# Loading r and k of a chunk by heads (48 rows of 4 KB twice) instead of by columns (112 rows of 2 KB twice)

## The chip, the cores and the metric

The kernel runs on one core of a Trainium2 chip. The metric is the time of one execution on the device in microseconds (us). A row of the traces is one instruction or a group of them on an engine: PE is TensorE (PEld its weight loads), DVE is VectorE, ACT is ScalarE, POOL is GpSimd and SP is SyncE. SP, ACT and POOL also issue DMAs; a name with a small q (SPq, ACTq) is the queue of instructions in front of the engine.

## The reference

A linear attention with decay (batch 4, 8 heads, 768 steps, 48 channels per head) feeds a mixture of 8 experts, of which each token takes one. In short:

```python
for t in range(S):                                   # S = 768
    kt, vt, rt = (k[:, :, t], v[:, :, t], r[:, :, t])
    cur = np.einsum('bhd,bhe->bhde', u[None] * kt, vt)
    y[:, :, t] = np.einsum('bhd,bhde->bhe', rt, state + cur)
    state = w[None, :, :, None] * state + np.einsum('bhd,bhe->bhde', kt, vt)
...
e_idx = np.argmax(x @ w_gate, axis=1)                # x: y as 3072 tokens x 384
for e in range(E):                                   # E = 8
    h = np.maximum(x[mask] @ w1[e], 0.0)
    out[mask] = gate_w[mask, None] * eom[mask, e, None] * (h @ w2[e])
```

## The kernel before

The attention goes through 24 chunks (NT) of 128 steps of one batch entry, six chunks of time (NCH) for each of the four batch entries, the entries in turn. Within a chunk the steps are two halves of 64 (c = 0, 1), and the 8 heads are 4 pairs (q) of two heads (j = 0, 1).

A chunk's input is one block of the array `rkv`: 128 rows of 1792 floats. The first 512 columns are r transposed, the next 512 are k transposed, and then follow k and v by tokens, 384 each. In the transposed part a row is a channel: rows 0 to 47 are the channels of the even heads (j = 0), rows 64 to 111 those of the odd heads (j = 1), and rows 48 to 63 and 112 to 127 are zeros. Along a row the order is half, pair, step.

The tiles called `rk` (128 x 1024 floats, 4 KB per row) hold r and k transposed of a chunk; there are five (`RINGS`), so chunk i uses tile i % 5. The tiles `k` (four) and `v` (five) hold the rest. Chunks 0 to 4 are loaded into `rk` in one DMA each of all 128 rows ahead of the loop. Each later chunk is loaded in two DMAs of `load`, which is told a part n: n = 0 is r and n = 1 is k, in both cases rows 0 to 111 (48 + 64). The second stays clear of the last 16 zero rows, which nobody overwrites with anything but zeros.

The order of the instructions on every engine is written out by hand, and each engine takes them in that order. In iteration i of the loop (from L1479):

- POOL multiplies r and k of chunk i + 2 (`product`), and DVE scales r and k of chunk i + 3 by a table in place (`scale`, L297).
- PE does `strips` of chunk i + 1; then ACT issues the load of part 0 of chunk i + 5 (L1488) and the load of `k` of chunk i + 5 (L1493), and later the store of a finished chunk.
- PE does `intra` of chunk i (L399), after which SP issues the load of `v` of chunk i + 5 (L1513).
- PE does `state` of chunk i + 2 (L353), `scores` of chunk i + 1 for three pairs (L327, called at L1517), `inter` of chunk i + 1 (L389, L1520) and `scores` for the fourth pair (L1521). `scores` reads r and k, `inter` reads r.
- SP issues the load of part 1 of chunk i + 6 (L1528).

So both parts of a chunk are issued one after the other, part 1 at the end of one iteration and part 0 early in the next. Ahead of the loop SP issues part 1 of chunk 5 (L1459), behind `scores(0)`, `product(0)` and `inter(0)`. The routing of finished chunks (small steps on DVE and PE) is woven into the same iterations. Behind the attention the experts run one after the other, with PE as the busy engine; they use other tiles and other loads.

Of the kernel before, what the change touches and what calls it, by code (L numbers as in the profile page):

```python
# [20 lines left out]
B, H, S, D = 4, 8, 768, 48  # L21
C = 128
# [25 lines left out]
HB = 64  # L48
# [10 lines left out]
RINGS = {"rk": 5, "k": 4, "v": 5}  # L59
# [1219 lines left out]
def rwkv_top1_moe(ctx, tc, rkv, wu, wg, w1, w2, r, kk, v, w, u, out):  # L1279
# [11 lines left out]
    with ExitStack() as actx:  # L1291
# [6 lines left out]
        rings = {nm: [pin.tile([C, RKW if nm == "rk" else NAT], F32, name=f"{nm}_{n}") for n in range(RINGS[nm])] for nm, (a, z) in PARTS.items()}  # L1298

        def load(nm, i, n=None, eng=nc.sync):  # L1300
            if i < NT:
                a, z = PARTS[nm]
                rows, at = slice(0, C), 0
                if n is not None:
                    rows, at, a, z = slice(0, HB + D), 512 * n, a + 512 * n, a + 512 * (n + 1)
                eng.dma_start(rings[nm][i % RINGS[nm]][rows, at : at + z - a], rkv[i, rows, a:z])

        for nm, i in (("rk", 0), ("k", 0), ("rk", 1), ("v", 0), ("k", 1), ("rk", 2), ("v", 1), ("k", 2)):
            load(nm, i)
# [14 lines left out]
        for nm, i in (("v", 2), ("rk", 3), ("k", 3), ("v", 3), ("rk", 4), ("v", 4)):  # L1324
            load(nm, i)
# [126 lines left out]
        make_fold(tc, rw, k)  # L1452
        att.state(0)
        load("k", RINGS["k"])
        att.causal(0)
        att.carry(0, 0)
# [195 lines left out]
```

## Time and profile before

| | us |
|---|---|
| median of three runs | 376.56 |
| lowest and highest of them | 375.86, 376.89 |
| the profiled execution | 372.32 |
| its span, first to last instruction | 370.5 |
| granted clock of TensorE, mean over the span | 0.98 of full |

The page lists the busy time of each engine and then cuts the span into 40 slices of 9.3 us. Each digit is the busy share of a slice in tenths. A wait is put down to what ended it; "issue" means that the engine waited for nothing that the profile shows. DMA shares are shares of 16 DMA engines' time. Times in timelines and windows are us from the start of the span.

### The profile page before, as it was taken

To read this page: it belongs to the slowest core of one execution; us is meant where nothing else is said; L and a number is where in the kernel's file an instruction comes from. 1 tells how busy PE (TensorE), PEld (TensorE's weight loads), DVE (VectorE), ACT (ScalarE), POOL (GpSimd) and SP (SyncE) were. 2 spreads that over 40 slices of the span, in tenths; PEclk is the share of its full clock that TensorE was granted. 3 is DMA by queue.
4 is the path that set the end of the run, shared out by engine and by line. 5 is a ranking of instruction groups with operands and counts; after the bars stand their busy time and mean duration, and the time that the engine had idled before them with its cause. 6 is when DMAs were issued, how large, how long until landed. Compare 5 with 4: busy or idle time off the path is not lost. (4 is left out here: it accounts for less than half of the span.)

```text
span 370.5 us, 12089 instructions
## 1 busy us (share of the span) xinstructions
PE 339.0 (92%) x4821; PEld 313.7 (85%) x4821; DVE 208.3 (56%) x481; ACT 179.0 (48%) x542; POOL 156.6 (42%) x229
## 2 busy tenths in 40 slices
PE   6699888889889889899999999999999999999990
PEld 2587776778777779889999999999999999999990
DVE  6566666857858428666446616624834835736500
ACT  3476654645646754265346434615535545535400
POOL 4968766746657575426005215223122132411021
PEclk9999999989989999999999999999999999999997
DMA  7968767767784351637526435633633734835010
GB/s 268 322 188 259 217 188 211 237 175 222 222 248 152 103 168 40 233 93 229 185 84 197 138 103 160 203 103 100 218 128 113 231 127 128 294 108 153 15 48 21
DMA packets 28850, 61.40 MB, mean 166 GB/s; under 512 B 4157, under 2 KB 13395, under 8 KB 28784
## 3 DMA queue, kind: packets, MB, share of 16 engines
q1 hardware_dynamic: 17120, 38.29, 33.2%
q10 hardware_dynamic: 8336, 12.60, 10.8%
q0 software_dynamic: 3328, 9.64, 8.2%
q8 instruction: 40, 0.66, 0.7%
q14 instruction: 26, 0.21, 0.2%
HBM read 51.04 MB, written 9.70 MB: 164 GB/s over the span
## 5 line engine op out<-in xcount | busy, mean ns | idle before, releaser
L896 POOL DMA_INDIRECT out_dram<-yo,gi x28 | 29.8, 1063 | 107.4 <-ACT yo L893 41.6
L858 PE MATMUL ps_h<-xh,w1h 128*128 128x416 f32 (+6 forms) x192 | 65.5, 341 | 0.0
L859 PE MATMUL ps_h<-xl,w1h 128*128 128x416 f32 (+6 forms) x192 | 63.7, 332 | 0.0
L860 PE MATMUL ps_h<-xh,w1l 128*128 128x416 f32 (+6 forms) x192 | 63.6, 331 | 0.0
L772 DVE TENSOR_TENSOR w1l<-raw,w1h 128x768 fp32r<-128x768 f32 x28 | 26.2, 957 | 62.1 <-ACT w1h L771 62.1
L807 POOL DMA_INDIRECT xg<-x_d,gi x28 | 30.8, 1099 | 55.7 <-PE ps_z L881 40.1
L867 ACT ACTIVATE hh<-ps_h 128x416 fp32r<-128x416 f32 (+6 forms) x64 | 30.8, 484 | 33.9 <-PE ps_h L860 33.7
L414 ACT ACTIVATE vc<-v,cs 128x48 f32<-128x48 f32 x192 | 45.9, 322 | 0.1
L868 DVE SCALAR_TENSOR_TENSOR hl<-ps_h,hh 128x416 fp32r<-128x416 f32 (+6 forms) x64 | 34.3, 540 | 15.7 <-ACT hh L867 15.6
L858 PEld LDWEIGHTS ps_h<-xh,w1h 128*128 128x128 f32 x192 | 36.1, 188 | 0.3
L859 PEld LDWEIGHTS ps_h<-xl,w1h 128*128 128x128 f32 x192 | 36.2, 188 | 0.0
L860 PEld LDWEIGHTS ps_h<-xh,w1l 128*128 128x128 f32 x192 | 36.1, 188 | 0.0
L373 POOL TENSOR_TENSOR T<-Ts,sq 128x192 f32<-128x192 f32 x40 | 20.3, 508 | 35.4 <-DVE Ts L372 20.5
L879 PE MATMUL ps_z<-hh,w2h 128*128 128x416 f32 (+2 forms) x96 | 33.7, 351 | 0.0
L399 PE MATMUL ps_y<-v,A 64*64 64x64 f32 x768 | 30.0, 227 | 4.0 <-issue 2.6
L881 PE MATMUL ps_z<-hh,w2l 128*128 128x416 f32 (+2 forms) x96 | 33.3, 347 | 0.0
L880 PE MATMUL ps_z<-hl,w2h 128*128 128x416 f32 (+2 forms) x96 | 33.3, 347 | 0.0
L921 PE MATMUL ps_o<-w2h,hh 128*128 128x384 f32 (+2 forms) x96 | 32.9, 343 | 0.0
L923 PE MATMUL ps_o<-w2h,hl 128*128 128x384 f32 (+2 forms) x96 | 32.2, 336 | 0.0
L922 PE MATMUL ps_o<-w2l,hh 128*128 128x384 f32 (+2 forms) x96 | 32.2, 336 | 0.0
L399 PEld LDWEIGHTS ps_y<-v,A 64*64 64x64 f32 x768 | 26.0, 139 | 5.9 <-issue 3.8
L310 POOL TENSOR_TENSOR rk<-rk 128x512 f32<-128x512 f32 x24 | 30.5, 1273 | 0.0
(214 smaller groups left out, 693.1 us busy)
## 6 DMA issues: line engine op xcount, KB each, us to landing
raw<-in_w_dram SPq DMA_DIRECT2D x64, 384.0 KB, 3.3
v<-in_rkv_dram SPq DMA_DIRECT2D x24, 192.0 KB, 4.2
x_d<-x ACTq DMA_DIRECT2D x22, 200.0 KB, 3.4
rk<-in_rkv_dram SPq DMA_DIRECT2D x19, 224.0 KB, 3.4
rk<-in_rkv_dram ACTq DMA_DIRECT2D x19, 224.0 KB, 3.5
k<-in_rkv_dram ACTq DMA_DIRECT2D x19, 192.0 KB, 3.7
rk<-in_rkv_dram SPq DMA_DIRECT2D x5, 512.0 KB, 5.3
k<-in_rkv_dram SPq DMA_DIRECT2D x5, 192.0 KB, 5.2
```

Source lines behind the costliest of these rows:

```text
L399: nc.tensor.matmul(o, A[rows, j, q, :], self.values(i, rows, 2 * q + j), start=(i < B and c == 0 and q == 0), stop=(q == NP - 1), skip_gro ...
L414: nc.scalar.activation(vc[:, h, :], vt[:, h, :], AF.Copy, scale=cs[:, h : h + 1])
L858: nc.tensor.matmul(o, wh[:, j, fs], xh, start=(j == 0), stop=False)
L859: nc.tensor.matmul(o, wh[:, j, fs], xl, start=False, stop=False)
L860: nc.tensor.matmul(o, wl[:, j, fs], xh, start=False, stop=(j == KC - 1))
L868: nc.vector.scalar_tensor_tensor(hl, o, 0.0, hh, op0=ALU.max, op1=ALU.subtract)
L879: nc.tensor.matmul(o, wh, hh, start=(f == 0), stop=False)
L880: nc.tensor.matmul(o, wh, hl, start=False, stop=False)
L881: nc.tensor.matmul(o, wl, hh, start=False, stop=(f == FC - 1))
L921: nc.tensor.matmul(o, hh, wh, start=(f == 0), stop=False)
L922: nc.tensor.matmul(o, hh, wl, start=False, stop=False)
L923: nc.tensor.matmul(o, hl, wh, start=False, stop=(f == FC - 1))
```

## The change

Part n of `load` becomes a block of rows in place of a block of columns: n = 0 is rows 0 to 47 (the even heads) with both r and k, 4 KB per row, and n = 1 is rows 64 to 111 (the odd heads). The zero rows 48 to 63 are no longer written behind the first load of a tile; they keep their zeros. The number of DMAs, the engines that issue them and their places in the order stay.

```diff
         def load(nm, i, n=None, eng=nc.sync):
             if i < NT:
                 a, z = PARTS[nm]
-                rows, at = slice(0, C), 0
+                rows = slice(0, C)
                 if n is not None:
-                    rows, at, a, z = slice(0, HB + D), 512 * n, a + 512 * n, a + 512 * (n + 1)
-                eng.dma_start(rings[nm][i % RINGS[nm]][rows, at : at + z - a], rkv[i, rows, a:z])
+                    rows = slice(HB * n, HB * n + D)
+                eng.dma_start(rings[nm][i % RINGS[nm]][rows, : z - a], rkv[i, rows, a:z])
```

Here C is 128, HB is 64 and D is 48.

## Rows read from the trace of the kernel before

**Rows 1.** The page: busy time, and slices of PE and DMA.
```profile
PE 339.0 (92%) x4821; PEld 313.7 (85%) x4821; DVE 208.3 (56%) x481; ACT 179.0 (48%) x542; POOL 156.6 (42%) x229
...
PE   6699888889889889899999999999999999999990
...
DMA  7968767767784351637526435633633734835010
```

**Rows 2.** Windows: stretch, its length, busy per engine, clock, DMA share, GB/s.
```profile
20.00:33.00 13.00, 12.94 (x417) 10.98 (x413) 9.64 (x17) 9.17 (x41) 10.34 (x33) 1.00 0.77 234
33.00:107.00 74.00, 64.35 (x2123) 55.20 (x2123) 50.21 (x113) 41.60 (x191) 49.64 (x71) 0.97 0.72 217
107.00:127.00 20.00, 18.31 (x563) 15.78 (x558) 14.21 (x37) 12.90 (x58) 11.69 (x13) 0.95 0.46 146
```

**Rows 3.** PE's waits, 33 to 107 us (us, times, longest): first and last.
```profile
PE ps_cf L405 <- issue: 2.8, 2, 1.7
...
PE ps_y L389 <- issue: 0.4, 1, 0.4
```

**Rows 4.** PE's waits, 107 to 130 us: the longest.
```profile
PE ps_y L399 <- DVE A L333: 1.2, 2, 0.8
```

**Rows 5.** PE's timeline: start, duration, instruction, [idle before, ended by].
```profile
42.53 0.33 PE L399 MATMUL ps_y<-v,A 64*64 64x64 f32 x3
43.82 0.97 PE L399 MATMUL ps_y<-v,A 64*64 64x64 f32 x26 [0.96 <-issue]
...
78.36 0.65 PE L405 MATMUL ps_cf<-rk,uw 128*32 128x128 f32 x8 [1.69 <-issue]
...
104.67 0.55 PE L486 MATMUL ps_x<-ident,x 128*128 128x128 f32 x3 [1.21 <-issue]
```

**Rows 6.** DMA queues, 20 to 103 us: packets, MB, share of 16 engines.
```profile
q10 hardware_dynamic: 6928, 10.52, 40.5%
q1 hardware_dynamic: 4582, 7.20, 30.2%
q8 instruction: 19, 0.31, 1.6%
```

**Rows 7.** Windows around two drops of the granted clock.
```profile
78.30:81.70 3.40, 3.34 (x43) 2.86 (x45) 1.06 (x2) 1.64 (x9) 2.34 (x3) 0.50 0.39 121
...
104.50:109.00 4.50, 4.33 (x108) 4.30 (x109) 1.35 (x4) 2.96 (x13) 2.01 (x2) 0.62 0.94 270
```

**Rows 8.** SP's timeline, 10 to 20 us.
```profile
11.31 0.37 SPq L1306 DMA_DIRECT2D rk<-in_rkv_dram  x1
16.18 0.34 SPq L1306 DMA_DIRECT2D v<-in_rkv_dram  x1
19.77 0.33 SPq L1306 DMA_DIRECT2D rk<-in_rkv_dram  x1
```

**Rows 9.** Line 1306 on ACT: duration in ns, minimum, median, maximum.
```profile
L1306 ACTq EVENT_SEMAPHORE  x36: 17/17/38, 14.8 to 105.3; - x36
L1306 ACTq DMA_DIRECT2D rk<-in_rkv_dram x19: 334/334/390, 14.9 to 103.6; - x19
```

**Rows 10.** SP's waits, 10 to 108 us (us, times, longest).
```profile
SPq L1306 <- PE ps_a L327: 26.4, 17, 3.1
```

**Rows 11.** PE's timeline at inter(0).
```profile
12.02 0.68 PE L389 MATMUL ps_y<-T,rk 48*64 48x64 f32 x16 [1.24 <-DVE T L368]
```

**Rows 12.** ACT's timeline, second half of chunk 6.
```profile
20.17 0.33 ACTq L1306 DMA_DIRECT2D rk<-in_rkv_dram  x1
```

**Rows 13.** DVE's timeline, scale of chunk 6.
```profile
28.63 1.22 DVE L297 TENSOR_TENSOR rk<-rk,ps_tb 128x1024 f32<-128x1024 f32 x1
```

**Rows 14.** Tile rk, 13 to 107 us: time from issue to landing.
```profile
DMA to landing us min/median/max: 2.5/3.5/4.6
```

**Rows 15.** Line 297 (scale): idle before it (us, times) until this.
```profile
  DMA rk<-in_rkv_dram: 0.2, 1
```

**Rows 16.** DMA queues, 3 to 8 us: packets, MB, share of 16 engines.
```profile
q1 hardware_dynamic: 788, 1.92, 99.0%
```

## The prediction

> **What bounds the kernel now.** The page comes first [rows 1]. TensorE (PE) is busy 92% of the 370.5 us, but the slices differ: the first 18 hold 6 to 9 tenths, the others are full but for the last. All r and k loads are issued before 104 us, in the first twelve slices, so only idle time of PE in that stretch can change. The DMA slices are highest in the same stretch.
>
> Next come the windows [rows 2]. From 20 to 33 us PE is busy 12.94 of 13.00 us; from 33 to 107 us 64.35 of 74.00; from 107 to 127 us 18.31 of 20.00. The DMA shares are 0.77, 0.72 and 0.46. In the middle stretch every wait of PE is "issue", an engine that waits for nothing that the profile shows: 12 waits in six rows, 9.5 us [rows 3]. Behind 107 us none of PE's waits is of that kind; the longest is for DVE [rows 4]. The last reloads are issued at 103 us and land a few us later, so these waits end with the loads. One of them looks like this: PE stands idle 0.96 us in the middle of L399's matmuls, whose inputs were there for the three before [rows 5].
>
> The DMA view gives a candidate for what PE waits for. In 83 us queue q8, of kind "instruction", moved 19 packets of 0.31 MB in all, 16 kB each [rows 6]. PE's two rows in the middle stretch are 2123 instructions each, 4246 in 74 us [rows 2], and 19 packets in 83 us make 17 in 74 us: about 250 instructions to a packet. I read the 12 waits as instruction packets that come late because they share the 16 DMA engines with the loads. That is an inference from coincidence: from 20 to 33 us the DMA share was as high and PE waited for nothing.
>
> The Trainium skill, page "Runtime: NRT & Kernel Launch", section "Instruction fetch mechanics", says that instructions are refilled in 16 KiB blocks of 256 and that crossing a block is mostly hidden. The packet size agrees with the 16 kB of [rows 6]; "mostly hidden" does not agree with the 9.5 us of [rows 3], if my reading of them is right. By that rule the change would be worth nothing at all, 376.6 us; by the rows it is worth what the sum below says.
>
> PE's clock is part of it. From 78.3 to 81.7 us the granted clock was 0.50, the lower level of 1.2 GHz, and from 104.5 to 109 us it was 0.62 on average [rows 7]. Each drop follows an "issue" wait, of 1.69 us until 78.36 and of 1.21 us until 104.67 [rows 5], and costs 3.4 x 0.50 = 1.7 us and 4.5 x 0.38 = 1.7 us.
>
> **The change part by part.** *Issue.* 38 transfers before, 38 after, on the same queues at the same places: on SP the issues took 0.37 and 0.33 us for the 112 rows of rk and 0.34 us for the 128 of v [rows 8], on ACT a median of 334 ns for rk [rows 9], so no price by rows is visible. Nothing.
>
> *Waits of the transfers.* SP's reload at L1528 now overwrites r and k of one head of each pair instead of k of both. The last reader of either is the same: scores' last matmuls (L1521), behind inter (L1520). SP waits for that matmul already, 17 times, 26.4 us in all [rows 10]. ACT's reload finds its slot free: its semaphore instructions take 38 ns at most [rows 9]. Only the first SP reload (L1459) gains a wait: it was issued at 11.31 us, and inter(0), which reads r, starts at 12.02 and takes 0.68 us [rows 8, 11]. It moves by about 1.4 us; behind it on SP stands the v load, which waits for its own release until 16.18 us, so nobody is held up. Nothing.
>
> *Landing.* The shortest way from the second half's issue to its first reader is chunk 6: ACT issues at 20.17 us, scale reads at 28.63 us [rows 12, 13], 8.5 us, against 3.5 us median and 4.6 us at most to land [rows 14]. Scale waited for an rk transfer once in the whole execution, 0.2 us [rows 15]. So 3.9 us cover the slowest one; gone, each us would cost up to a us per chunk.
>
> *DMA work.* Per chunk 2 x 112 rows x 2048 B = 458.8 kB become 2 x 48 x 4096 = 393.2 kB, and 224 packets become 96. Over 20 to 103 us ACT's queue q10 took 40.5% of 16 engines for 10.52 MB, SP's q1 30.2% for 7.20 MB [rows 6]: 51.1 and 55.7 ns of one engine per kB. The reload costs 229.4 x (51.1 + 55.7) = 24.5 engine-us per chunk; at the same price per kB it will cost 21.0. All queues together spend about 960 engine-us on 17 chunks, 56.5 each, so the change takes 3.5, or 6%. No row shows a transfer into 48 partitions, so the price per kB has bounds. Low: the opening burst, where 4 KB rows are mixed with others, 99% of 16 engines x 5 us for 1.92 MB [rows 16], 41.3 ns per kB: 16.2 engine-us, -8.3 per chunk. High: each transfer now lands on one half of the partitions; if each half has ways of its own, and half the engines' rate goes through them, the price doubles: 42.0, +17.5. I take the middle value, the same queues' own price: both halves are issued 0.4 us apart (19.77 and 20.17 us [rows 8, 12]) and run side by side, so together they fill the partitions as before.
>
> *What PE gets of it.* 9.5 us of waiting at a DMA share of 0.72 and none at 0.46 make 36.5 us per unit of share [rows 2, 3]. A cut of 6% of 0.72 is 0.045: -1.6 us. From below it is 0, since 0.77 went without a wait for 13 us. I take the middle, -0.8 us.
>
> **The sum.** The profiled execution took 372.32 us, 1.8 us more than its span; less 0.8 it is 371.5. The three timed runs have a median of 376.56, 4.2 us above that execution, so executions of this kernel differ by more than the term; for the median the sum gives 375.8. A measurement of this kernel tells about 0.3% (1.1 us) from no change, so this is no measurable change.
>
> **The rivals.**
> *Faster: the waits shrink with the work.* For it: the waits end where the loads end [rows 3, 4]. Against: no wait at 0.77 [rows 2]. At the full slope -1.6 us; at the low price 15% of 0.72, -3.9 us; a clock drop that no longer comes gives 1.7 us more. 371 to 375 us. Chance 0.33.
>
> *Slower: half the partitions, dearer packets.* Its place is each reload between 20 and 107 us. From 62.3 ns per kB on (24.5 / 393.2), 17% above the loop's 53.4, the reload costs more engine time than before, and instruction packets come later. At half as much again: 31.5 engine-us, +12%, +3.3 us, and one more clock drop, 1.7 us: 381.6. Doubled: +31%, +8.1 us, 384.7. For it: nothing in the trace lands on so few partitions. Against: the halves overlap. Chance 0.23.
> Here the Trainium skill speaks against the change: "SBUF — State Buffer", section "Door 1: The DMA port swizzle", says that DMA bandwidth goes by how many of 16 ports the partitions reach, and that partitions 0 to 63 reach 8, 64 to 127 the other 8. No transfer here shows it. By it alone each half would take the doubled price, 384.7 us.
>
> *Slower: other drops.* Shifted packets make another long wait, and the clock falls once or twice more with no more DMA work: +1.7 to +3.4 us. Chance 0.05.
>
> *Slower: scale waits for a late half.* The landing would have to go from 3.5 to over 8.5 us; then up to a us per chunk for each us. Chance 0.02.
>
> **How the numbers follow.** No measurable change 0.37 (the likeliest; own range 375.4 to 377.7), faster 0.33, slower 0.23 + 0.05 + 0.02 = 0.30. The range goes from 372.8, a low price without a clock gain, to 380.5, most of the way to half as much again: it leaves out about one in ten on each side.
>
> **What would show it.** q1 and q10 lose 19 x 64 packets each, and 1.2 MB together. Scale still waits for no reload. The DMA share from 33 to 107 us is about 0.68; over 0.75 speaks for dearer packets, and the time to landing with it. PE's "issue" waits in that stretch stay within 8 to 10 us, with two clock drops. The prediction is wrong if these waits move by 2 us or more, if a drop goes or comes, or if waits appear on rk's landing.

## The result and the profile after

The changed kernel takes 376.75 us (median of 22 executions, 373.05 to 379.94) against 375.86 (369.56 to 380.73), a ratio of 1.0068 with a 95% interval of 1.0041 to 1.0094. The comparison leaves out every execution more than 1.5% above the fastest of its own kernel, which takes more from the kernel before because one of its executions took 369.56; over all 22 of each the medians differ by 0.24%. A second comparison on another chip gave 1.0030, 0.9990 to 1.0071. The change makes the kernel slower by something between nothing and 0.9%; a gain of more than 0.1% is excluded.

The forecast of 375.8 us started from three runs of the kernel before with a median of 376.56; over 22 executions that median is 375.86. So the forecast stood for 0.8 us less, and the kernel came out 0.9 us slower by the medians of all executions, some 2.6 us by the ratio.

The profiled execution of the changed kernel took 373.06 us, with a span of 371.1. PE and DVE execute as many instructions as before; only the two rk transfers have another shape. Its windows over the same stretches as [rows 2], with the same columns:

```profile
20.00:33.00 13.00, 12.71 (x410) 10.79 (x410) 9.21 (x16) 8.94 (x41) 10.53 (x34) 1.00 0.83 222
33.00:107.00 74.00, 64.82 (x2159) 55.27 (x2162) 50.33 (x113) 41.78 (x192) 49.52 (x71) 0.98 0.74 203
107.00:127.00 20.00, 17.28 (x528) 14.51 (x532) 13.96 (x36) 13.87 (x61) 12.54 (x14) 1.00 0.47 152
```

In the middle stretch fewer bytes move (203 GB/s for 217) and yet the DMA engines are busier, 0.74 for 0.72, where the prediction said about 0.68; from 20 to 33 us 0.83 for 0.77. The DMA queues from 20 to 103 us, beside [rows 6], say which:

```profile
q10 hardware_dynamic: 5833, 9.96, 44.4%
q1 hardware_dynamic: 3526, 6.67, 28.6%
```

The share times 16 engines times 83 us, divided by the bytes, is 59.2 ns of one engine per kB on ACT's queue, where it was 51.1, and 56.9 on SP's, where it was 55.7; for both queues together 58.3 for 53.0. A second execution of the changed kernel (after_again, below) gives 59.4 for both. Over the whole execution the page counts 64 packets fewer for each of 19 transfers on either queue (before: 17120 on q1 and 8336 on q10):

```profile
q1 hardware_dynamic: 15904, 37.67, 33.2%
q10 hardware_dynamic: 7120, 11.98, 11.7%
```

PE's waits from 33 to 107 us (us in all, times, longest), beside [rows 3]. All that are "issue":

```profile
PE ps_cf L405 <- issue: 3.4, 2, 2.0
PE ps_y L399 <- issue: 2.7, 5, 0.9
PE ps_a L353 <- issue: 1.4, 4, 0.8
PE ps_x L486 <- issue: 1.0, 1, 1.0
PE ps_y L389 <- issue: 0.7, 1, 0.7
```

That is 9.2 us in 13 waits, where the kernel before had 9.5 in 12. But the same view from 107 to 130 us now holds two rows of this kind, where the kernel before had none [rows 4]:

```profile
PE ps_y L389 <- issue: 1.5, 2, 1.2
PE ps_cf L500 <- issue: 0.9, 1, 0.9
```

With 0.2 us from 20 to 33 us this makes 11.8 us instead of 9.5. Summed from 8 to 140 us it is 12.1 for 10.3, and 11.1 in after_again. PE's clock still falls twice to its lower level of 1.2 GHz, the first time at the same place as in [rows 7], the second time later (the middle window shows the place where it fell before):

```profile
78.30:81.70 3.40, 3.22 (x39) 2.74 (x40) 0.64 (x2) 1.01 (x6) 1.90 (x2) 0.51 0.24 63
104.50:109.00 4.50, 3.86 (x127) 3.42 (x127) 2.59 (x8) 3.08 (x13) 3.16 (x4) 1.00 0.99 266
129.60:133.00 3.40, 3.40 (x40) 2.83 (x39) 1.63 (x8) 2.40 (x8) 0.76 (x2) 0.51 0.85 273
```

SP's timeline, beside [rows 8], has the first reload 1.3 us later and the v load behind it where it was:

```profile
12.61 0.34 SPq L1306 DMA_DIRECT2D rk<-in_rkv_dram  x1
16.03 0.34 SPq L1306 DMA_DIRECT2D v<-in_rkv_dram  x1
19.07 0.33 SPq L1306 DMA_DIRECT2D rk<-in_rkv_dram  x1
```

### The profile page after: what moved, and what is told of

The parts are those of the page before. It is cut to its first block, busy times and chain, and to the rows that moved or that the text cites. A ratio compares the mean times of both kernels' runs of the same rounds, so it can differ in the third digit from the quotient of the medians.

```text
span 371.1 us, 12073 instructions
## 1 busy us (share of the span) xinstructions
PE 340.3 (92%) x4821; PEld 314.1 (85%) x4821; DVE 208.6 (56%) x481; ACT 179.5 (48%) x542; POOL 158.0 (43%) x229
## 5 line engine op out<-in xcount | busy, mean ns | idle before, releaser
L807 POOL DMA_INDIRECT xg<-x_d,gi x28 | 31.6, 1127 | 54.9 <-PE ps_z L881 39.1
L310 POOL TENSOR_TENSOR rk<-rk 128x512 f32<-128x512 f32 x24 | 30.5, 1273 | 0.0
```

## The experiments

Theory 1 is the prediction's "half the partitions, dearer packets": a transfer into neighbouring rows of one half of the partitions costs more DMA time per byte, and instruction packets then reach PE later. Against it stand theory 2 (long packets: the size or number of the transfers costs), theory 3 (packets cost by their bytes and the difference is scatter), and the place of issue. Ratios are to the kernel before on the same chip, with 95% intervals; where the medians of all executions tell something else, they stand beside. In the edits HB is 64 and D is 48, and of long edits only the lines that matter are shown.

**micro: the transfers by themselves.** Nothing of the kernel is computed: only transfers run, eight of each shape from SP, then eight pairs of each from SP and ACT. All of a shape go into one place of one tile, so that on each queue one waits for the one before it. Rows and columns of part n:

```
cols:   slice(0, HB + D), slice(512 * n, 512 * (n + 1))     # 112 rows x 2 KB
heads:  slice(HB * n, HB * n + D), slice(0, RKW)            # 48 x 4 KB
rows:   slice(HB * n, HB * (n + 1)), slice(0, RKW)          # 64 neighbouring x 4 KB
step:   slice(n, C, 2), slice(0, RKW)                       # every second x 4 KB
all:    slice(0, C), slice(512 * n, 512 * (n + 1))          # 128 x 2 KB
```

> Transfers alone, nothing of the kernel's computation: for each of five shapes (112 rows x 2 KB, 48 rows x 4 KB, 128 rows x 2 KB, 64 rows x 4 KB taking every second row, 64 neighbouring rows x 4 KB), eight transfers one after the other from SP, then eight pairs of halves from SP and ACT at once. Theory 1 (half the partitions make packets dearer): 48 neighbouring rows alone take about twice the engine time per byte of 112 rows or of every second row, and 64 neighbouring rows likewise; in pairs the gap shrinks but stays. Theory 2 (long packets): 4 KB packets cost as much per byte as 2 KB packets in every shape. Theory 3 (scatter): as theory 2.

Some of the DMA issues of this program (tile, engine, count, KB each, median us from issue to landing):

```profile
all<-in_rkv_dram SPq DMA_DIRECT2D x8, 256.0 KB, 2.6
step<-in_rkv_dram SPq DMA_DIRECT2D x8, 256.0 KB, 2.9
rows<-in_rkv_dram SPq DMA_DIRECT2D x8, 256.0 KB, 3.4
...
cols<-in_rkv_dram SPq DMA_DIRECT2D x8, 224.0 KB, 2.6
...
heads<-in_rkv_dram SPq DMA_DIRECT2D x8, 192.0 KB, 2.8
```

These are the transfers one by one. For the same 256 KB, 64 spread rows take 0.3 us longer than 128 rows, and 64 neighbouring rows another 0.5. The 192 KB of 48 neighbouring rows land later than the 224 KB of 112. The DMA queues while the pairs run, first the two columns parts (124.81 to 148.05 us), then the two halves of heads (149.50 to 174.34 us):

```profile
q1 hardware_dynamic: 1024, 1.84, 26.9%
q10 hardware_dynamic: 1024, 1.84, 24.4%
...
q1 hardware_dynamic: 512, 1.57, 23.9%
q10 hardware_dynamic: 512, 1.57, 23.0%
```

Both queues' share times 16 engines times the stretch, over both queues' bytes, is 51.8 ns per kB for the columns and 59.4 for the heads: 15% more. Of 256 KB each, 64 neighbouring rows side by side cost 60.0 and 64 spread rows 51.5. Alone, from SP only, the columns cost 54.9, the heads 55.8, 64 neighbouring rows 56.1 and 64 spread rows 57.1 ns per kB, so theory 1's expectation of twice the price alone was missed. The higher price is one of two concentrated transfers side by side, which is how the loop runs them.

The rule of the Trainium skill that spoke against the change ("SBUF — State Buffer", section "Door 1: The DMA port swizzle": fewer ports reached, less bandwidth) agrees in the order of the landings, 3.4 us for 64 neighbouring rows against 2.6 for 128. Of the prediction's doubled price per kB nothing is seen in the engines' time: 60.0 ns against 51.5 is the widest gap in micro. The landing itself can't rule a doubling out, because most of it does not go with the bytes, as one transfer of the kernel before shows:

```profile
wu<-in_wu_dram SPq DMA_DIRECT2D x1, 4.0 KB, 1.9
```

Less these 1.9 us, 1.5 us stand against 0.7 (an estimate, from one transfer of 4 KB).

**cols128, heads64, step2: 128 rows' bytes in three shapes.** All three load the same 512 KB per chunk in two transfers, issued where the changed kernel issues its own.

```
cols128 (kernel before):  rows ... = slice(0, HB + D), ...   ->  slice(0, C), ...
heads64 (changed kernel): rows = slice(HB * n, HB * n + D)   ->  slice(HB * n, HB * n + HB)
step2   (changed kernel): rows = slice(HB * n, HB * n + D)   ->  slice(n, C, 2)
```

> The kernel before with all 128 rows of 2 KB in both parts (65.5 kB more per chunk). Theory 1: all partitions, so packets at 84 to 110 ns; engine time per chunk rises at most by the bytes, 14% of the reload; time within 0.3% of before. Theory 2: short packets, time as before. Theory 3: as before.

> The changed kernel with 64 rows of 4 KB per part instead of 48. Theory 1: as dear per byte as the changed kernel and a third more bytes, so ratio to before 1.005 to 1.015. Theory 2: 4 KB packets as in the changed kernel, ratio about 1.007. Theory 3: 1.000.

> Each part takes every second row of all 128, 64 rows of 4 KB: the same packets and bytes as 64 neighbouring rows, but on partitions of both halves. Theory 1: packets near 160 to 180 ns, ratio to before 1.000 within 0.003 or less than 1. Theory 2: as with 64 neighbouring rows, about 1.007. Theory 3: 1.000.

Measured: cols128 1.0042 (1.0005 to 1.0080), step2 1.0081 (1.0043 to 1.0118), heads64 1.0235 (1.0182 to 1.0288). Between heads64 and step2 only the partitions differ, neighbouring or spread, and that is worth 1.5%: theory 2 and theory 3, by which the two are equal, are excluded as its cause. 64 spread rows are within 0.4% of the columns of the same bytes (cols128). So theory 1's mechanism is shown at 64 rows, but not its figures: heads64 lies above its range, and step2, which it put within 0.3% of before or faster, is 0.8% slower, which is what theory 2 said. At 48 rows in the changed kernel, 1.0068, no gap to step2 is seen. In heads64 PE's "issue" waits from 8 to 140 us sum to 15.3 us (before 10.3, step2 12.4), and the clock falls for longer. Windows of heads64 around two of its drops:

```profile
52.60:59.40 6.80, 6.19 (x139) 5.70 (x142) 1.34 (x5) 2.85 (x13) 2.12 (x4) 0.50 0.46 130
114.00:124.20 10.20, 9.82 (x181) 9.18 (x182) 4.68 (x11) 5.87 (x27) 5.03 (x6) 0.50 0.65 187
```

In 17.0 us at half the clock it loses 8.5. PE's timeline of heads64 just before the first:

```profile
53.21 0.43 PE L405 MATMUL ps_cf<-rk,uw 128*32 128x128 f32 x3 [2.50 <-issue]
```

PE had stood idle for 2.50 us until 53.21, and the granted clock is at its lower level from about there on.

**loads_on: do PE's "issue" waits hang on the loads?** The kernel before, whose loads go on after the last chunk into tiles that nobody reads.

```
-            if i < NT: ... eng.dma_start(rings[nm][i % RINGS[nm]][...], rkv[i, rows, a:z])
+            t = rings[nm][i % RINGS[nm]] if i < NT else rest[nm]
+            eng.dma_start(t[rows, at : at + z - a], rkv[i % NT, rows, a:z])
```

> The kernel before, whose loads go on behind the last chunk: iterations 18 to 23 load again the first chunks into tiles that nobody reads. Theory 1 (PE's issue waits are instruction packets held up by the loads): between 107 and 130 us issue waits come back, 3 to 5 of 0.3 to 1.2 us, 2 to 4 us in all, and the kernel is slower by 2 to 5 us (ratio 1.005 to 1.013). Rival (the waits end at 107 us because PE then waits for DVE anyway): no issue waits there, ratio 1.000 within 0.003.

Measured: 1.0119 (1.0069 to 1.0170). PE's longest waits from 107 to 130 us, where before had none for issue [rows 4]:

```profile
PE ps_y L389 <- issue: 2.5, 3, 1.2
```

With the same work on PE and more loads the kernel is slower, as theory 1 expected. That these waits are the price of the added loads is not shown. Two of the three stand at a place of the program where the changed kernel waits too, 20 us after its last issue of a load of r, k or v; PE's timeline there, changed kernel, then loads_on:

```profile
126.88 0.46 PE L389 MATMUL ps_y<-T,rk 48*64 48x64 f32 x15 [1.15 <-issue]
127.69 0.50 PE L389 MATMUL ps_y<-T,rk 48*64 48x64 f32 x17 [0.35 <-issue]
...
128.96 0.56 PE L389 MATMUL ps_y<-T,rk 48*64 48x64 f32 x19 [1.15 <-issue]
129.78 0.42 PE L389 MATMUL ps_y<-T,rk 48*64 48x64 f32 x11 [0.27 <-issue]
```

cols128 and `one` (below) have this pair of waits as well; only the third one in loads_on, 1.07 us, may be the loads'. And the edit does one thing more: the added k loads all go into one tile, so that ACT waits for the one before, twice, 3.4 us in all. The prediction's reading stays an inference here; the twins bear on it better.

**twin_cols, twin_heads: SP's part loaded twice.** The kernel before and the changed one, each with an extra copy into a tile that nobody reads.

```
+                if n == 1:
+                    eng.dma_start(twin[rows, ...], rkv[i, rows, a:z])
```

> The kernel before with SP's part loaded twice, the second time into a tile that nobody reads: 112 rows x 2 KB, 229 kB more per chunk. Theory 1: more DMA work in the loop (about 12 engine-us per chunk, a fifth more), more issue waits, ratio 1.005 to 1.03. Rival: waits do not hang on the DMA work, ratio 1.000 within 0.003.

> The changed kernel with SP's part loaded twice in the same way: 48 rows x 4 KB, 197 kB more per chunk. Theory 1 (rows on half of the partitions make their own and the other queue's packets dearer): in spite of 33 kB less in the twin, and 98 kB less per chunk in all, slower than the twin by columns by 0.5 to 2%. Rival (bytes decide): faster than the twin by columns by 0.3 to 1%.

Measured: 1.0316 (1.0260 to 1.0373) and 1.0305 (1.0253 to 1.0357). A third transfer costs 3%, in "issue" waits (17.1 and 17.5 us from 8 to 140 us, before 10.3) and in clock (0.91 and 0.88 of full in that stretch, before 0.97). The extra copies go into one tile, so SP waits for the one before, 6.2 and 5.6 us in all; PE's added waits are for nothing that the profile shows. But the two kernels do not differ, though the heads move 98 kB less per chunk. Theory 1 had expected the heads to be 0.5 to 2% slower, the rival by bytes 0.3 to 1% faster: neither was met. That fewer bytes into neighbouring rows cost as much as more bytes in columns lies between the two. The DMA share from 8 to 140 us is 0.82 for the heads and 0.75 for the columns at equal waits, so the share doesn't set the waits by itself.

**one: one transfer of 128 rows x 4 KB.** The changed kernel with no transfer from ACT.

```
-                if n is not None:
-                    rows = slice(HB * n, HB * n + D)
+                if n == 0:
+                    return
```

> One transfer per chunk of all 128 rows x 4 KB, from SP, in the place of its part; ACT issues none for r and k. Theory 1 (it is the half of the partitions that is dear): packets of 4 KB near 160 to 200 ns, 524 kB per chunk at 52 ns per kB or 27 engine-us against 24.5 of before, ratio to before 0.997 to 1.005. Theory 2 (long packets hold up instruction packets): as dear as the change, 1.007 or more.

Measured: 373.57 us, 0.9948 (0.9913 to 0.9982): faster than both kernels, with more bytes than either. Theory 2's 1.007 is excluded; theory 1's range, 0.997 to 1.005, is reached by the interval only. Its window of the middle stretch:

```profile
33.00:107.00 74.00, 64.98 (x2205) 55.15 (x2203) 51.21 (x119) 41.64 (x195) 49.96 (x72) 1.00 0.76 234
```

The DMA share is higher than in the changed kernel, 0.76 against 0.74, and the clock doesn't fall here. So a higher share need not cost time. Why this kernel is faster its trace doesn't say: its "issue" waits from 8 to 140 us sum to 10.7 us, before to 10.3.

The Trainium skill, page "DMA: Bandwidth & Descriptors", section "Rules for kernel authors", advises one transfer over 128 partitions instead of two into halves; this run agrees. The page's reason, that the two serialize, is not what micro shows: eight pairs of 64 neighbouring rows took 29.74 us (227.47 to 257.21), eight single ones 27.18 (96.18 to 123.36).

**after_again, heads_sp, cols_sp, one112: place and number of transfers at 48 and 112 rows.** after_again is the changed kernel unedited. The "_sp" kernels (changed kernel and kernel before) issue both parts from SP at one place; one112 is a single transfer of 112 rows x 4 KB.

```
_sp:     -            load("rk", i + RINGS["rk"], 0, nc.scalar)
         +            load("rk", i + 1 + RINGS["rk"], 0)      # behind the same line with 1
one112:  rows = slice(HB * n, HB * n + D)  ->  n == 0: return;  n == 1: slice(0, HB + D)
```

> The changed kernel once more, beside new runs of the kernel before. Theory 1 (half of the partitions makes the packets dearer, a little over the bytes saved): ratio 1.002 to 1.007. Rival (no difference, the first comparison was scatter): 1.000 within 0.003.

> The changed kernel with both halves issued from SP, one after the other (ACT issues none of r and k). Theory 1: the halves follow one another in one queue, so that each is alone on its half of the partitions: no better than the changed kernel, 1.003 to 1.015 against before. Rival (the gain of the one transfer of 128 rows comes from sparing ACT the issue): faster than before by 0.3 to 0.8%.

> The kernel before with both parts issued from SP, one after the other. Theory 1: all partitions in either part, so as before or, if sparing ACT the issue is what helped the one transfer, 0.3 to 0.8% faster; in any case faster than the changed kernel with both halves on SP by 0.5% or more. Rival (bytes and packets decide): slower than that one by 0.3% or equal.

> One transfer per chunk from SP of 112 rows x 4 KB: 459 kB against 524 kB of the one transfer of 128 rows. If bytes decide: faster than the 128 rows by 0.2 to 0.5%, ratio to before 0.990 to 0.994. If an even share of partitions per engine decides (128 rows over 16 engines): not faster than the 128 rows, 0.995 to 1.003.

Measured: after_again 1.0030 (0.9990 to 1.0071), heads_sp 1.0004 (0.9950 to 1.0058), cols_sp 1.0049 (1.0008 to 1.0090), one112 0.9952 (0.9910 to 0.9994). Over all 12 executions of each the medians stand to before as 1.0045 for heads_sp and 1.0034 for cols_sp. Either way, on one queue, where the two halves are issued one behind the other, no gap between heads and columns is seen; theory 1 had expected 0.5% or more. after_again decides nothing: its interval holds both 1.000 and the 1.0068 of the first comparison. one112 is not faster than `one`, so the fewer bytes gain nothing there. one112 moves the bytes of cols_sp from the same place and is about 1% faster: it has one transfer for two and rows of 4 KB for 2 KB.

**heads64_sp, step2_sp, quarters_sp: what of it is neighbouring rows, and what the number.** The edit "_sp" on heads64, on step2, and on the kernel before with each part cut into two by columns:

```
quarters_sp:  for m in range(2 if n is not None else 1):      # four transfers of 112 x 1 KB
                  h = (z - a) // (2 if n is not None else 1)
                  eng.dma_start(rings[...][rows, at + m * h : at + (m + 1) * h], ...)
```

> 64 neighbouring rows x 4 KB per half, both halves from SP one after the other. If neighbouring rows are dear by themselves: ratio to before 1.012 to 1.025, and 0.8% or more above the spread rows on SP. If only two concentrated halves in two queues at once are dear: 1.000 to 1.010, equal to the spread rows on SP within 0.4%.

> Every second row, 64 x 4 KB per part, both from SP. If the length of packets is what makes one transfer faster: 0.994 to 1.000. If the number of transfers does: 1.003 to 1.010, as two transfers by columns on SP.

> By columns, in four transfers of 112 rows x 1 KB per chunk from SP, same bytes as one transfer of 112 x 4 KB. If number of transfers or packets matters: slower than two transfers on SP by 0.5% or more, ratio to before 1.008 to 1.02. If neither: 1.000 to 1.005.

Measured: heads64_sp 1.0236 (1.0185 to 1.0286), step2_sp 0.9998 (0.9958 to 1.0039), quarters_sp 1.0057 (1.0017 to 1.0098). By the medians of all executions they are 1.0199, 1.0060 and 1.0081. At 64 rows the price of neighbouring rows stays when both come from SP: 2.4% by the ratios, 1.4% by the medians. It falls on other transfers too. ACT's queue loads no `rk` in either of these kernels, and yet its packets are dearer beside the neighbouring rows; from 20 to 103 us, heads64_sp, then step2_sp:

```profile
q10 hardware_dynamic: 4320, 6.01, 27.8%
q10 hardware_dynamic: 4464, 6.22, 21.2%
```

That is 61.4 ns per kB against 45.3, and the loads of `k` on that queue land after 4.6 us against 3.6. At 48 rows (heads_sp) it is 56.7, against 51.9 in cols_sp. Four transfers of 1 KB rows (quarters_sp) cost between nothing and 0.5% more than two of 2 KB rows (cols_sp), so no price that grows evenly with number or row length is seen. step2_sp and one112 differ by 0.5%, by 1.0% in the medians; whether one transfer or its rows make the gain isn't settled.

## Why the prediction was wrong, step by step

**The bound**, "issue" waits of PE that grow with the loads, is borne out by the twins, 17.1 and 17.5 us for 10.3. That the waits end with the loads is not: the changed kernel has 1.5 us of them 20 us behind its last such load, at a place where cols128 and `one` have them too. That they are late instruction packets was an inference and stays one.

**Issue, waits of the transfers and landing: nothing.** Right for PE. The first SP reload moved by 1.3 us (1.4 forecast) and the v load behind it was issued at 16.03 us against 16.18. What the prediction had not looked at is ACT's issue of the k load behind its rk: it took a median of 787 ns (702 in after_again), where it was 395; in heads_sp, where ACT issues no rk, 334. PE's waits from 33 to 107 us name no instruction of ACT, so no cost is seen. An rk transfer landed after a median of 3.6 us in after_again, against 3.5 before. Scale's idle time for rk in the changed kernel (us, times) answers to [rows 15]; one wait remains:

```profile
  DMA rk<-in_rkv_dram: 0.3, 1
```

**DMA work: the step that failed.** The packets went away as counted. But the middle value, "at the same price per kB", and its ground, that the two halves "together fill the partitions as before", did not hold. Two concentrated halves side by side, with no other transfer in flight, cost 15% more per kB. In the loop, q1 and q10 together went from 70.7% to 73.0% of 16 engines over 83 us: 30.5 engine-us more over 17 chunks, or 1.8 per chunk where 3.5 less was forecast. If the other loads kept their price, the reload costs 24.5 + 1.8 = 26.3 engine-us for 393.2 kB, 66.9 ns per kB, just above the 62.3 from which the slower rival decides. The queues of heads_sp and cols_sp show that other transfers get dearer too, so this is the most that the reload itself can cost by these traces, and micro gives 59.4. What is shown is that the loads together cost more, not less: the slower rival's direction, near its lower end, and far from the doubled price.

**What PE gets of it: the slope failed too.** Its lower point, no wait at a share of 0.46, was a matter of one execution: from 107 to 130 us the changed kernel has 2.4 us at 0.49, cols128 1.7 at 0.44. By the slope, 0.02 more share would be +0.7 us. The "issue" waits from 20 to 130 us grew by 2.3 us in one execution of each, from 8 to 140 us by 1.8, or 0.8 in after_again, and the medians differ by 0.9 us. The sign fits, no more. From 33 to 107 us, where the prediction had its sign of being wrong, they stayed at 9.2 us, within the 8 to 10 named; the added ones came behind, and 1.5 us of them so late that the dearer transfers can't have been in flight any more. The slope does not carry further: twin_heads and twin_cols wait equally at shares 0.82 and 0.75, and one is faster at 0.76.

**The clock.** Two drops, as forecast; the second moved from 104.5 to 129.6 us and cost no more. In this execution no further drop made the kernel slower.

**What stays open.** That the price per kB of the loads rose at 48 rows is shown, in two executions of the changed kernel, in micro's pairs and in heads_sp. That the whole 0.7% comes from it is only argued: executions of the changed kernel differ by more than that, the second comparison gave 1.0030, heads_sp against cols_sp shows no gap, and most of the added waits stand where the transfers were over. Shown for time is the same mechanism at 64 rows, where the rows' spread alone is worth 1.5% (heads64 against step2) and 1.4 to 2.4% on SP.

## What to carry to other kernels

A cut in bytes that narrows a transfer to neighbouring partitions may buy nothing: here 14% fewer bytes came with about 15% more engine time per byte when two such transfers ran side by side, and with no gain in time. One transfer over all partitions was the best of the shapes tried (0.995), even with bytes that nobody reads. Cost such a change by the transfer in the company that it has in the loop, since alone the two shapes had nearly the same price (54.9 and 55.8 ns per kB), and look at what the other queues pay.

## What the runs showed of the hardware

Two transfers into neighbouring partitions of either half, side by side, cost more engine time per kB than two of the same bytes into spread partitions (60.0 ns against 51.5), and in the loop they make the packets of another queue dearer (61.4 against 45.3).

PE waits for nothing that the profile shows in 9 to 18 us of the stretch from 8 to 140 us, and a third transfer per chunk brought the most of it (17.1 and 17.5 us for 10.3). That it is instruction packets which come late fits this, but no run showed one packet and one wait together. A long wait of that kind can be followed by a drop of the granted clock to 1.2 GHz which costs about as much again or more: in the kernel before, waits of 1.69 and 1.21 us were followed by losses of 1.7 us each, and in heads64 one of 2.50 us came with a drop of 6.8 us, a loss of 3.4. It need not be: in `one` a wait of 2.0 us stood between 33 and 107 us, and the clock was 1.00 there.
